# Four small edits to a planned attention and gated-FFN kernel: v transfers cut the other way, set-up work moved between engines, the pooled softmax scaled on ScalarE, the first block's weight remainders on VectorE

## The chip, the cores and the metric

One core of one Trainium2 chip runs the whole program. The time is device microseconds of one execution. The kernel before was timed three times: 1013.88, 1006.59 and 1011.54 us, median 1011.54 us. A profiled execution has a time of its own, and its trace is what the rows below come from.

## The reference, cut to what matters

```python
# q, k, v: [4 batches, 8 heads, 576 positions, 64], float32
q_d, k_d, v_d = means over groups of 4 positions            # 144 pooled positions
out_d  = softmax(q_d @ k_d.T / 8) @ v_d                      # pooled attention
out_up = repeat(out_d, 4 times along the positions)
scores = where(|i - j| < 4, q @ k.T / 8, -1e9)               # band of 7 positions
x = out_up + softmax(scores) @ v                             # -> [2304 tokens, 512]
x = (sigmoid(x @ w_gate) * (x @ w_val)) @ w_out              # 512 -> 1536 -> 512
h = x @ w_in                                                 # 512 -> 2048
out = (h * sigmoid(1.702 * h)) @ w_out2                      # 2048 -> 512
```

The weights come as 64-bit floats. All sums must hold float32 accuracy.

## The kernel before

The tokens are cut into five blocks: block b (0 to 3) is the first 512 positions of batch b, and block 4 gathers the last 64 of all four batches. TensorE multiplies in a fast format that does not hold a whole float32, so every operand of a dense product is split into a high part and a remainder ("hi" and "lo"), and each product is three matmuls (L710 to L712): hi by hi, lo by hi, hi by lo.

The work before each of blocks 0 to 3 is the attention of that batch, cut into four jobs (one for each pair of heads, `Job`). A job loads q and k transposed (`load`), pools them on GpSimd (`pool4`, L462 and L464), forms the scores of the band on TensorE (L494), does their softmax on VectorE and ScalarE (L501 to L521), and does the pooled attention: scores on TensorE (L534), maxima on VectorE (L541), exponentials with their sums on ScalarE (L549), the inverse of the sums on VectorE (L556, L557), the scaling by it on GpSimd (L561, two instructions a job, each of 72 x 288 elements), a transpose on TensorE against an identity matrix `ident` (L575), and a copy on ScalarE (L580). Then TensorE multiplies the band (L603) and the pooled part (L611) by the values, and `combine` makes the two parts of x.

Two jobs share one half of the value columns (`Values`, eight halves in all). A half is loaded twice. `vg` holds groups of four rows on 72 partitions, two transfers of 288 KB, and VectorE sums them (L431, L433). `vt` holds windows of 32 rows, 24 windows as 4 quarters of the partitions by 6 columns: window number 6i+g lies in partitions 32i to 32i+31, column g. It is loaded in six transfers: one for each quarter of the partitions (32 partitions by 6, or 5, columns), and one each for the first and the last window, which stand partly outside the sequence and are cut short.

The first layer's weights are made out of 64-bit words while block 0 is computed. For each of 36 tiles of 128 x 512, `bits` scales the upper words (L657 on VectorE for the first few, L659 on ScalarE after that), and shifts and joins the halves on VectorE (L661, L663); `signed` puts the sign in (L668, VectorE). The float32 tile stays on the chip. `parts_of` then makes the two parts: ScalarE rounds to hi (L674), and GpSimd or VectorE subtracts it (L676). In block 0 all 36 remainders are GpSimd's; in blocks 1 to 3 the third part of each step is VectorE's, and in block 4 every second tile.

The order is fixed when the program is built. Each piece of work is put down with its engine, a length in ns, what it reads and writes, and a due time (`op`); `Plan.order` walks through a simple model of five engines, gives each engine the ready piece that is due first, and emits the instructions in that order. Each engine runs its own instructions strictly in the order in which they were emitted, and the SP queue issues all the transfers in its order. Where the planner sees TensorE idle early, it puts in filler matmuls (L882).

The set-up at the start is not planned: `memset`s for padding and constants, a band mask made on GpSimd (L336 to L347), and `ident`, are emitted ahead of all planned work, in the order of the source.

Of the kernel before, what the change touches and what calls it, by code (L numbers as in the profile page):

```python
# [10 lines left out]
F32 = mybir.dt.float32  # L11
# [8 lines left out]
P = 128  # L20
# [41 lines left out]
class Plan:  # L62
# [29 lines left out]
    def op(self, eng, ns, fn, reads=(), writes=(), due=0.0, after=0.0):  # L92
        o = Op()
        o.eng, o.ns, o.fn, o.due, o.n, o.ready = eng, ns, fn, due, len(self.ops), after
        o.fresh, o.bufs = [], set()
        deps = set()
        for group, writing in ((reads, False), (writes, True)):
            for x in group:
                b, part = x if isinstance(x, tuple) else (x, None)
                assert b.some or b.slot.last is b  # L100
                if b.some:
                    o.bufs.add(b)
                    if not b.log:
                        o.fresh.append(b)
                new = True
                for p, q, w in b.log:
                    if (w or writing) and (part is None or q is None or part == q):
                        deps.add(p)
                        new = new and not w
                if new:  # L110
                    for x in b.before:
                        deps.update(e[0] for e in x.log)
        for group, writing in ((reads, False), (writes, True)):
            for x in group:
                b, part = x if isinstance(x, tuple) else (x, None)
                b.log.append((o, part, writing))
        deps.discard(o)
        o.deps = deps
        self.ops.append(o)
        return o  # L120
# [97 lines left out]
def tile_multiscale_attention_gated_ffn(  # L218
# [9 lines left out]
    nc = tc.nc  # L228
    B, NHP, _, S = qT.shape
    D = 64  # L230
    DM = v.shape[2]
# [3 lines left out]
    G = S // 4  # L235
    GH = G // 2
# [14 lines left out]
    NQ, NU = 24, 30  # L251
    NT = S // NQ
    NG = NT // 4
    VC = 2 * P
    HALF = S // 2

    sb = ctx.enter_context(tc.tile_pool(name="sb", bufs=1))
# [5 lines left out]
    op, buf = plan.op, plan.buf  # L263
# [13 lines left out]
    KPAD = 3  # L277
# [25 lines left out]
    qslots, kslots, vslots, pslots = (plan.rings[nm][0] for nm in ("qt", "kt", "vt", "pt"))  # L303
# [23 lines left out]
    warm = sb.tile([P, P], BF16, name="warm", tag="warm")  # L327
    nc.vector.memset(warm, 0.0)
    for s in qslots:
        nc.gpsimd.memset(s.t[:, S:], 0.0)  # L330
    for s in kslots:
        nc.gpsimd.memset(s.t[:, :KPAD], 0.0)
        nc.gpsimd.memset(s.t[:, KPAD + S:], 0.0)
    mask = sb.tile([P, NG, NU], F32, name="mask", tag="mask")
    band = sb.tile([P, NU], F32, name="band", tag="band")
    nc.gpsimd.memset(band, 0.0)  # L336
    for i in range(4):
# [7 lines left out]
                            fill=NEG, base=-3, channel_multiplier=0)  # L345
    nc.gpsimd.affine_select(out=mask[96:, NG - 1], in_=mask[96:, NG - 1], pattern=[[-1, NU]],
                            compare_op=ALU.is_ge, fill=NEG, base=S + 2 - NQ * (NT - 1), channel_multiplier=0)  # L347
    for s in vslots:
        nc.gpsimd.memset(s.t[:32, 0], 0.0)
        nc.gpsimd.memset(s.t[96:, NG - 1], 0.0)  # L350
    ident = sb.tile([P, P], F32, name="ident", tag="ident")
    make_identity(nc, ident)
    for s in pslots:
        nc.vector.memset(s.t, 0.0)


    def act_ns(n, psum=False):
# [8 lines left out]
    def dma(out_, in_, nbytes, reads, writes, due, after=0.0):  # L366
        op("sp", nbytes, lambda: nc.sync.dma_start(out=out_, in_=in_), reads, writes, due, after)
# [32 lines left out]
    class Values:  # L400
# [6 lines left out]
        def load(self):  # L407
            b, c = self.b, slice(self.c0, self.c0 + VC)
            self.vg, self.vt, self.vd = buf("vg"), buf("vt"), buf("vd")

            hp = self.job.hp
            d, after = (self.job.t0 - 3000.0, self.job.t0 - 12000.0) if b else (4500.0 * hp, 4500.0 * hp)
            for kh in range(2):
                dma(self.vg.t[:, kh], v[b, kh * 4 * GH:(kh + 1) * 4 * GH, c].rearrange("(g r) d -> g r d", r=4),
                    GH * 4 * VC * 4, [], [(self.vg, kh)], d, after)
            d, after = (self.job.due(0.2), self.job.t0 - 9000.0) if b else (4500.0 * hp + 3000.0, 6000.0 * hp)
            for i in range(4):
                g0, g1 = i == 0, NG - (i == 3)
                row = NQ * (NG * i + g0) - 3
                src = v[b, row:row + 32, c]  # L420
                src = bass.AP(tensor=src.tensor, offset=src.offset,
                              ap=[[DM, 32], [NQ * DM, g1 - g0], [1, VC]])
                dma(self.vt.t[32 * i:32 * i + 32, g0:g1], src, 32 * (g1 - g0) * VC * 4, [], [(self.vt, i)], d, after)
            dma(self.vt.t[3:NU, 0], v[b, :NU - 3, c], (NU - 3) * VC * 4, [], [(self.vt, 4)], d, after)
            row = NQ * (NT - 1) - 3
            dma(self.vt.t[96:96 + S - row, NG - 1], v[b, row:S, c], (S - row) * VC * 4, [], [(self.vt, 5)], d, after)

        def pool(self):
            vg, vd = self.vg, self.vd
# [6 lines left out]
    class Job:  # L436
# [88 lines left out]
        def down(self):  # L525


            ss = [Buf(None, self.banks) for _ in range(2)]
            qd, kd, nmd, smd, pd = self.qd, self.kd, self.nmd, self.smd, self.pd

            def pe():
                for r in range(2):
                    for h in range(2):
                        nc.tensor.matmul(ss[h].t[:GH, r * G:(r + 1) * G],  # L534
                                         qd.t[h * D:(h + 1) * D, r * GH:(r + 1) * GH],
                                         kd.t[h * D:(h + 1) * D, :], start=True, stop=True)

            at = self.due(0.5)
            op("pe", 560.0, pe, [qd, kd], [*ss, nmd, (smd, 0), (smd, 1), (pd, 0), (pd, 1)], at)
            for h in range(2):  # L540
                op("dve", dve_ns(2 * G), lambda h=h: nc.vector.reduce_max(  # L541
                    nmd.t[:, 2 * h:2 * h + 2], ss[h].t[:GH, :2 * G].rearrange("p (r k) -> p r k", k=G), axis=AX.X),
                   [ss[h]], [(nmd, h)], at)
            op("dve", 90.0, lambda: nc.vector.tensor_scalar_mul(nmd.t, nmd.t, -SCALE_D), [], [nmd], at)

            def ex(h):
                for r in range(2):
                    x = 2 * h + r
                    nc.scalar.activation(pd.t[:, h, r], ss[h].t[:GH, r * G:(r + 1) * G], AF.Exp,  # L549
                                         bias=nmd.t[:, x:x + 1], scale=SCALE_D, accum_out=smd.t[:, x:x + 1])  # L550

            for h in range(2):
                op("act", 1100.0, lambda h=h: ex(h), [nmd, ss[h]], [(pd, h), (smd, h)], at)

            def inv():
                nc.vector.tensor_scalar_add(smd.t, smd.t, 1.0e-9)  # L556
                nc.vector.reciprocal(smd.t, smd.t)  # L557

            op("dve", 305.0, inv, [], [smd], at)
            for h in range(2):  # L560
                op("pool", 680.0, lambda h=h: nc.gpsimd.tensor_mul(  # L561
                    pd.t[:, h], pd.t[:, h], smd.t[:, 2 * h:2 * h + 2, None].to_broadcast([GH, 2, G])),
                   [smd], [(pd, h)], at)

        def down_t(self):
            self.pdt = buf("pdt")
            ss = [Buf(None, self.banks) for _ in range(2)]
            pd, pdt = self.pd, self.pdt

            def pe():  # L570
                for h in range(2):
                    for kh in range(2):
                        for r in range(2):
                            o = kh * G + r * GH
                            nc.tensor.transpose(ss[h].t[:GH, o:o + GH], pd.t[:, h, r, kh * GH:(kh + 1) * GH],  # L575
                                                ident[:GH, :GH])

            op("pe", 500.0, pe, [(pd, 0), (pd, 1)], [*ss, (pdt, 0), (pdt, 1)], self.due(0.65))
            for h in range(2):
                op("act", 370.0, lambda h=h: nc.scalar.copy(  # L580
                    pdt.t[:, h], ss[h].t[:GH, :2 * G].rearrange("p (k q) -> p k q", q=G)),
                   [ss[h]], [(pdt, h)], self.due(0.65))
# [98 lines left out]
    def weights(vi, f, part, t):  # L681

        if vi["layer"] == 2:
            return wt[2, f, part]
        if vi["j"] == 0:
            w32[f, part] = buf("w")
            signed(*bits(1, f, part, t - 8000.0), w32[f, part], t - 8000.0)
        hi, lo = buf("whi"), buf("wlo")
        nsplit[0] += 1
        eng = "pool"  # L690
        if vi["j"] == E:
            eng = ("pool", "dve")[nsplit[0] % 2]
        elif vi["j"] > 0 and part == 2:
            eng = "dve"
        parts_of(w32[f, part], hi, lo, t - 4000.0, eng)
        return hi, lo
# [225 lines left out]
```

## Time and profile before

| | |
|---|---|
| three runs, median | 1011.54 us (1006.59 to 1013.88) |
| profiled execution, its own time | 1016.06 us |
| its span | 1014.2 us |
| TensorE busy | 970.4 us, 96% |
| VectorE busy | 524.7 us, 52% |
| ScalarE busy | 395.6 us, 39% |
| GpSimd busy | 309.1 us, 30% |
| mean granted TensorE clock | 0.967 of full speed |

Busy times are shares of the whole span, and the stages differ much: the attention and the making of the weights stand in the first fifth, the two layers' matmuls fill the rest. A row of a stage says more than the table. PE is TensorE's matmuls, PEld its weight loads, DVE VectorE, ACT ScalarE, POOL GpSimd, SP the queue that issues the transfers. In the chain of waits, "issue" is time in which an engine waited for nothing that the profile shows.

### The profile page before, as it was taken

To read this page: it belongs to the slowest core of one execution; us is meant where nothing else is said; L and a number is where in the kernel's file an instruction comes from. 1 tells how busy PE (TensorE), PEld (TensorE's weight loads), DVE (VectorE), ACT (ScalarE), POOL (GpSimd) and SP (SyncE) were. 2 spreads that over 40 slices of the span, in tenths; PEclk is the share of its full clock that TensorE was granted. 3 is DMA by queue.
4 is the path that set the end of the run, shared out by engine and by line. 5 is a ranking of instruction groups with operands and counts; after the bars stand their busy time and mean duration, and the time that the engine had idled before them with its cause. 6 is when DMAs were issued, how large, how long until landed. Compare 5 with 4: busy or idle time off the path is not lost.

```text
span 1014.2 us, 18484 instructions
## 1 busy us (share of the span) xinstructions
PE 970.4 (96%) x7614; PEld 790.8 (78%) x7614; DVE 524.7 (52%) x886; ACT 395.6 (39%) x822; POOL 309.1 (30%) x290
## 2 busy tenths in 40 slices
PE   6597998999999999999999989999999999999997
PEld 5575776787777877888888987788888788888886
DVE  5679999545453554467565679723222222322232
ACT  2334444444444443455555655423213221312222
POOL 5266454644434543345444442102001100100000
PEclk7679897999999999999999999999999999999999
DMA  8654844350012410124203225102000100100010
GB/s 186 169 165 130 220 151 145 80 141 29 4 50 56 119 32 8 44 76 166 84 1 110 96 76 184 55 1 83 1 1 23 51 1 1 52 1 1 0 43 21
DMA packets 37270, 72.42 MB, mean 71 GB/s; under 512 B 5777, under 2 KB 17985, under 8 KB 37185
## 3 DMA queue, kind: packets, MB, share of 16 engines
q1 hardware_dynamic: 37184, 71.24, 24.7%
q8 instruction: 60, 0.98, 0.4%
q14 instruction: 26, 0.20, 0.1%
HBM read 61.26 MB, written 9.96 MB: 70 GB/s over the span
## 4 chain that ended last, share of the span: by engine, by line
PE 79%; DVE 11%; issue 4%; DMA 2%; ACT 1%; POOL 1%; SPq 0%; POOLq 0%; DVEq 0%; ACTq 0%
PE ph L710 15%; PE ph L711 14%; PE ph L712 14%; PE acc L710 10%; PE acc L711 10%; PE acc L712 10%; DVE we L663 3%; PE pa L603 2%; DMA vg<-v 2%; DVE we L668 1%; DVE we L661 1%; DVE w L668 1%; PE pa L534 1%; PE pa L494 1%; DMA w<-w 1%
## 5 line engine op out<-in xcount | busy, mean ns | idle before, releaser
L676 POOL TENSOR_TENSOR wlo<-w,whi 128x512 fp32r<-128x512 f32 x126 | 178.8, 1422 | 242.0 <-ACT whi L674 224.9
L746 DVE SCALAR_TENSOR_TENSOR th<-th,ph 128x512 f32<-128x512 f32 (+1 forms) x140 | 88.5, 632 | 303.9 <-ACT th L741 206.5
L710 PE MATMUL ph<-xhi,whi 128*128 128x512 f32 (+1 forms) x480 | 185.0, 386 | 3.4 <-ACT th L741 3.2
L711 PE MATMUL ph<-xhi,wlo 128*128 128x512 f32 (+1 forms) x480 | 181.0, 377 | 1.0 <-POOL wlo L676 1.0
L712 PE MATMUL ph<-xlo,whi 128*128 128x512 f32 (+1 forms) x480 | 180.4, 376 | 0.0
L741 ACT ACTIVATE th<-ph 128x512 f32<-128x512 f32 (+1 forms) x140 | 77.6, 554 | 256.3 <-PE ph L712 256.3
L674 ACT CAST whi<-w 128x512 fp32r<-128x512 f32 x180 | 111.1, 617 | 124.1 <-PE acc L712 54.0
L710 PE MATMUL ph<-xhi,w 128*128 128x512 f32 (+1 forms) x320 | 120.4, 376 | 1.1 <-DVE th L746 0.8
L750 DVE TENSOR_TENSOR glo<-th,ghi 128x512 fp32r<-128x512 f32 (+1 forms) x140 | 95.6, 683 | 48.7 <-ACT ghi L749 47.9
L711 PE MATMUL ph<-xhi,w 128*128 128x512 f32 (+1 forms) x320 | 119.3, 373 | 0.0
L712 PE MATMUL ph<-xlo,w 128*128 128x512 f32 (+1 forms) x320 | 119.2, 373 | 0.0
L711 PE MATMUL acc<-w,glo 128*128 128x512 f32 x288 | 114.7, 398 | 1.1 <-DVE glo L750 1.1
L710 PE MATMUL acc<-w,ghi 128*128 128x512 f32 x288 | 114.2, 397 | 1.5 <-ACT ghi L749 1.5
L712 PE MATMUL acc<-w,ghi 128*128 128x512 f32 x288 | 114.5, 397 | 0.0
L710 PEld LDWEIGHTS ph<-xhi,whi 128*128 128x128 f32 x480 | 92.7, 193 | 22.9 <-issue 3.9
L712 PEld LDWEIGHTS ph<-xlo,whi 128*128 128x128 f32 x480 | 92.8, 193 | 16.4 <-DVE xlo L637 0.2
L711 PEld LDWEIGHTS ph<-xhi,wlo 128*128 128x128 f32 x480 | 92.7, 193 | 15.7 <-POOL wlo L676 1.4
L749 ACT CAST ghi<-th 128x512 fp32r<-128x512 f32 (+1 forms) x140 | 80.6, 576 | 58.7 <-DVE th L746 56.2
L821 POOL TENSOR_TENSOR xlo<-st,xhi 128x512 fp32r<-128x512 f32 (+1 forms) x24 | 29.1, 1230 | 224.8 <-ACT xhi L819 224.8
L710 PE MATMUL acc<-ghi,whi 128*128 128x512 f32 (+1 forms) x240 | 90.8, 378 | 0.6 <-DVE ev L786 0.6
L711 PE MATMUL acc<-ghi,wlo 128*128 128x512 f32 (+1 forms) x240 | 88.7, 370 | 0.0
L712 PE MATMUL acc<-glo,whi 128*128 128x512 f32 (+1 forms) x240 | 88.4, 368 | 0.0
(99 smaller groups left out, 1305.4 us busy)
## 6 DMA issues: line engine op xcount, KB each, us to landing
w<-w SPq DMA_DIRECT2D x68, 512.0 KB
qt<-qT SPq DMA_DIRECT2D x16, 288.0 KB
kt<-kT SPq DMA_DIRECT2D x16, 288.0 KB
vg<-v SPq DMA_DIRECT2D x16, 288.0 KB
x2d<-ev SPq DMA_DIRECT2D x16, 256.0 KB
st<-x2d SPq DMA_DIRECT2D x16, 256.0 KB
out<-ev SPq DMA_DIRECT2D x16, 256.0 KB
vt<-v SPq DMA_DIRECT2D x16, 192.0 KB
```

The source lines that it names most:

```text
L603: nc.tensor.matmul(s.t[h * D:(h + 1) * D, q:q + NQ], vt.t[ks, g, v0 + h * D:v0 + (h + 1) * D], tt.t[ks, h, g, :NQ], start=True, stop=True, ...
L663: op("dve", 602.0, lambda: nc.vector.scalar_tensor_tensor(e.t, wv[:, :, 0], 29, e.t, op0=ALU.logical_shift_right, op1=ALU.bitwise_or), [w] ...
L674: op("act", 520.0, lambda: nc.scalar.copy(hi.t, m.t.bitcast(F32)), [m], [hi], due)
L676: op(eng, ns, lambda: on.tensor_sub(lo.t, m.t.bitcast(F32), hi.t.bitcast(F32)), [m, hi], [lo], due)
L710: nc.tensor.matmul(o, lhi, rhi, start=first, stop=False)
L711: nc.tensor.matmul(o, llo, rhi, start=False, stop=False)
L712: nc.tensor.matmul(o, lhi, rlo, start=False, stop=last)
L741: op("act", act_ns(n, True), lambda h=h: nc.scalar.activation(th.t[:, :n], h.t[:, :n], AF.Tanh, scale=0.5 if layer == 1 else 1.702 / 4.0), ...
L746: op("dve", dve_ns(n), lambda: nc.vector.scalar_tensor_tensor(th.t[:, :n], th.t[:, :n], 1.0, hb[-1].t[:, :n], op0=ALU.add, op1=ALU.mult), ...
L749: op("act", act_ns(n), lambda: nc.scalar.copy(gh.t[:, :n], th.t[:, :n]), [th], [gh], t)
L750: op("dve", dve_ns(n), lambda: nc.vector.tensor_sub(gl.t[:, :n], th.t[:, :n], gh.t[:, :n].bitcast(F32)), [th, gh], [gl], t)
L821: op("pool", pool_ns(n), lambda k=k, st=st: nc.gpsimd.tensor_sub(lo.t[:, k, :n], st.t[:, :n], hi.t[:, k, :n].bitcast(F32)), [st, (hi, k)], ...
```

## The change

Five places are touched.

1. The small `memset`s of the padding of q, k and v go from GpSimd to VectorE, and those of `pt` stand with them ahead of the mask.
2. `ident` becomes a planned piece of GpSimd's work with an early due time; until now it stood in the set-up. The transposes now read it as a planned buffer.
3. The four transfers of `vt` by quarters of the partitions become six by columns: each fills one column g on all 128 partitions (96 for the first and the last column). The two short ones stay. A half goes from six transfers of `vt` to eight, with the same bytes.
4. The scaling of the pooled softmax goes from two GpSimd instructions a job to four ScalarE instructions, each of 72 x 144 elements with one scale for each partition.
5. In block 0 all 36 remainders of the weights go from GpSimd to VectorE.

```diff
     for s in qslots:
-        nc.gpsimd.memset(s.t[:, S:], 0.0)
+        nc.vector.memset(s.t[:, S:], 0.0)
     for s in kslots:
-        nc.gpsimd.memset(s.t[:, :KPAD], 0.0)
-        nc.gpsimd.memset(s.t[:, KPAD + S:], 0.0)
+        nc.vector.memset(s.t[:, :KPAD], 0.0)
+        nc.vector.memset(s.t[:, KPAD + S:], 0.0)
+    for s in vslots:
+        nc.vector.memset(s.t[:32, 0], 0.0)
+        nc.vector.memset(s.t[96:, NG - 1], 0.0)
+    for s in pslots:
+        nc.vector.memset(s.t, 0.0)
...
-    for s in vslots:
-        nc.gpsimd.memset(s.t[:32, 0], 0.0)
-        nc.gpsimd.memset(s.t[96:, NG - 1], 0.0)
-    ident = sb.tile([P, P], F32, name="ident", tag="ident")
-    make_identity(nc, ident)
-    for s in pslots:
-        nc.vector.memset(s.t, 0.0)
+    ident = Buf(Slot(sb.tile([P, P], F32, name="ident", tag="ident")))
+    op("pool", 650.0, lambda: make_identity(nc, ident.t), [], [ident], -10.0e3)
...
-            for i in range(4):
-                g0, g1 = i == 0, NG - (i == 3)
-                row = NQ * (NG * i + g0) - 3
-                src = v[b, row:row + 32, c]
+            for g in range(NG):
+                i0, i1 = g == 0, 4 - (g == NG - 1)
+                src = v[b, NQ * (NG * i0 + g) - 3:NQ * (NG * i0 + g) + 29, c]
                 src = bass.AP(tensor=src.tensor, offset=src.offset,
-                              ap=[[DM, 32], [NQ * DM, g1 - g0], [1, VC]])
-                dma(self.vt.t[32 * i:32 * i + 32, g0:g1], src, 32 * (g1 - g0) * VC * 4, [], [(self.vt, i)], d, after)
+                              ap=[[NG * NQ * DM, i1 - i0], [DM, 32], [1, VC]])
+                dma(self.vt.t[32 * i0:32 * i1, g], src, 32 * (i1 - i0) * VC * 4, [], [(self.vt, g)], d, after)
...
+            def norm(h):
+                for r in range(2):
+                    x = 2 * h + r
+                    nc.scalar.mul(pd.t[:, h, r], pd.t[:, h, r], smd.t[:, x:x + 1])
+
             for h in range(2):
-                op("pool", 680.0, lambda h=h: nc.gpsimd.tensor_mul(
-                    pd.t[:, h], pd.t[:, h], smd.t[:, 2 * h:2 * h + 2, None].to_broadcast([GH, 2, G])),
-                   [smd], [(pd, h)], at)
+                op("act", 640.0, lambda h=h: norm(h), [smd], [(pd, h)], at)
...
         eng = "pool"
         if vi["j"] == E:
             eng = ("pool", "dve")[nsplit[0] % 2]
-        elif vi["j"] > 0 and part == 2:
+        elif vi["j"] == 0 or part == 2:
             eng = "dve"
```

## Rows read from the trace of the kernel before

**Rows 1.** Windows: us, each engine's busy time, granted clock, DMA share, GB/s.

```profile
0.00:57.00 57.00, 37.12 (x989) 32.16 (x989) 32.67 (x84) 16.20 (x55) 28.93 (x58) 0.69 0.76 186
70.00:180.00 110.00, 96.83 (x959) 75.03 (x959) 107.30 (x167) 53.73 (x116) 57.74 (x45) 0.91 0.55 160
200.00:300.00 100.00, 100.00 (x1153) 79.78 (x1153) 49.60 (x101) 42.53 (x98) 40.76 (x39) 1.00 0.19 48
```

**Rows 2.** Chain that ended last: start us, us, what; first 57 us.

```profile
10.83 5.11 issue
...
25.60 5.19 issue
...
33.28 3.71 issue
...
50.11 4.69 POOL pd L561
```

**Rows 3.** Windows between those waits, columns as in the first group.

```profile
0.00:10.80 10.80, 7.42 (x222) 6.76 (x223) 2.35 (x7) 1.28 (x1) 8.72 (x36) 0.87 0.86 190
10.80:25.60 14.80, 9.69 (x254) 8.27 (x251) 10.64 (x27) 5.03 (x21) 6.46 (x11) 0.63 0.90 184
25.60:33.30 7.70, 2.49 (x129) 2.31 (x128) 4.13 (x8) 0.63 (x2) 1.87 (x2) 0.69 1.06 289
```

**Rows 4.** Page: TensorE's line, and the instruction queue (packets, MB, share).

```profile
PE 970.4 (96%) x7614; PEld 790.8 (78%) x7614; DVE 524.7 (52%) x886; ACT 395.6 (39%) x822; POOL 309.1 (30%) x290
...
q8 instruction: 60, 0.98, 0.4%
```

**Rows 5.** Transfers by issue: queue, count, KB each.

```profile
vg<-v SPq DMA_DIRECT2D x16, 288.0 KB
...
vt<-v SPq DMA_DIRECT2D x16, 192.0 KB
```

**Rows 6.** Windows: two vg transfers alone; then vg and vt together.

```profile
41.00:43.00 2.00, 2.00 (x26) 1.62 (x22) 1.10 (x3) 0.00 (x0) 0.00 (x0) 0.69 0.74 218
...
108.50:113.50 5.00, 5.00 (x116) 3.76 (x115) 4.93 (x7) 1.59 (x3) 4.00 (x5) 1.00 1.05 149
```

**Rows 7.** Timeline: SP issues four weight tiles; VectorE first reads one.

```profile
22.75 4.96 SPq L367 DMA_DIRECT2D w<-w  x4
...
43.85 0.77 DVE L657 TENSOR_SCALAR we<-w 128x512 f32<-128x512 f32 x2
```

**Rows 8.** ScalarE by line, 57 to 190 us: busy us, mean ns, idle.

```profile
L549 ACT ACTIVATE pd<-pa,nmd 72x144 f32<-72x144 f32 x16 | 5.8, 371 | 4.3 <-DVE nmd L544 4.3
```

**Rows 9.** Timeline of GpSimd's set-up: first vt memset, first pooling.

```profile
4.21 0.30 POOL L349 MEMSET vt<- 32x256 f32 x1
...
6.17 0.67 POOL L462 TENSOR_TENSOR half<-qt 128x288 f32<-128x288 f32 x1
```

**Rows 10.** GpSimd and VectorE by line, 57 to 190 us.

```profile
L676 POOL TENSOR_TENSOR wlo<-w,whi 128x512 fp32r<-128x512 f32 x33 | 51.0, 1554 | 50.5 <-ACT whi L674 36.6 <-DVE th L746 7.7 <-DVE xlo L637 5.0
...
L668 DVE SCALAR_TENSOR_TENSOR w<-w,we 128x512 int32<-128x512 int32 x33 | 28.4, 860 | 0.2
L663 DVE SCALAR_TENSOR_TENSOR we<-w,we 128x512 int32<-128x512 int32 x33 | 27.7, 838 | 0.3
L661 DVE TENSOR_SCALAR we<-we 128x512 int32<-128x512 int32 x33 | 24.6, 746 | 0.7 <-ACT we L659 0.6
```

**Rows 11.** VectorE by line, 190 to 440 us.

```profile
L676 DVE TENSOR_TENSOR wlo<-w,whi 128x512 fp32r<-128x512 f32 x23 | 18.6, 807 | 0.0
...
L663 DVE SCALAR_TENSOR_TENSOR we<-w,we 128x512 int32<-128x512 int32 x1 | 0.7, 693 | 0.0
L661 DVE TENSOR_SCALAR we<-we 128x512 int32<-128x512 int32 x1 | 0.4, 427 | 0.5 <-ACT we L659 0.5
```

**Rows 12.** Waits, whole span (total, times, longest); ScalarE's cast, 57 to 190.

```profile
DVE wlo L676 <- ACT whi L674: 15.5, 13, 4.0
...
L674 ACT CAST whi<-w 128x512 fp32r<-128x512 f32 x33 | 20.3, 615 | 23.6 <-DVE w L668 14.0 <-PE ph L712 5.5 <-PE acc L712 4.1
```

More of the change, by code (lines that the diff above doesn't have):

```diff
@@ L416, in load @@
             d, after = (self.job.due(0.2), self.job.t0 - 9000.0) if b else (4500.0 * hp + 3000.0, 6000.0 * hp)
-            for i in range(4):
-                g0, g1 = i == 0, NG - (i == 3)
-                row = NQ * (NG * i + g0) - 3
-                src = v[b, row:row + 32, c]
+            for g in range(NG):
+                i0, i1 = g == 0, 4 - (g == NG - 1)
+                src = v[b, NQ * (NG * i0 + g) - 3:NQ * (NG * i0 + g) + 29, c]
                 src = bass.AP(tensor=src.tensor, offset=src.offset,
-                              ap=[[DM, 32], [NQ * DM, g1 - g0], [1, VC]])
-                dma(self.vt.t[32 * i:32 * i + 32, g0:g1], src, 32 * (g1 - g0) * VC * 4, [], [(self.vt, i)], d, after)
-            dma(self.vt.t[3:NU, 0], v[b, :NU - 3, c], (NU - 3) * VC * 4, [], [(self.vt, 4)], d, after)
+                              ap=[[NG * NQ * DM, i1 - i0], [DM, 32], [1, VC]])
+                dma(self.vt.t[32 * i0:32 * i1, g], src, 32 * (i1 - i0) * VC * 4, [], [(self.vt, g)], d, after)
+            dma(self.vt.t[3:NU, 0], v[b, :NU - 3, c], (NU - 3) * VC * 4, [], [(self.vt, NG)], d, after)
             row = NQ * (NT - 1) - 3
-            dma(self.vt.t[96:96 + S - row, NG - 1], v[b, row:S, c], (S - row) * VC * 4, [], [(self.vt, 5)], d, after)
+            dma(self.vt.t[96:96 + S - row, NG - 1], v[b, row:S, c], (S - row) * VC * 4, [], [(self.vt, NG + 1)],
+                d, after)
         def pool(self):
@@ L575, in pe @@
                             nc.tensor.transpose(ss[h].t[:GH, o:o + GH], pd.t[:, h, r, kh * GH:(kh + 1) * GH],
-                                                ident[:GH, :GH])
-            op("pe", 500.0, pe, [(pd, 0), (pd, 1)], [*ss, (pdt, 0), (pdt, 1)], self.due(0.65))
+                                                ident.t[:GH, :GH])
+            op("pe", 500.0, pe, [(pd, 0), (pd, 1), ident], [*ss, (pdt, 0), (pdt, 1)], self.due(0.65))
             for h in range(2):
```

## The prediction

> **What bounds the kernel now.** I read the windows by stage first. From 200 us on TensorE is busy 100.00 of 100 us at full clock, so whatever is won or lost before that is carried to the end unchanged [rows 1]. From 70 to 180 us VectorE is busy 107.30 of 110 us and TensorE 96.83: VectorE sets the pace there, and TensorE could save at most 13.2 us of idling. In the first 57 us no engine is full: TensorE works 37.12 us, VectorE 32.67. So there are two bounds, a start that waits, and a stage that VectorE fills.
>
> What the start waits for is in the chain of waits: three pieces called "issue", 5.11, 5.19 and 3.71 us, 14.0 in all, in which TensorE waits for no other engine, and then a scaling on GpSimd, 4.69 us [rows 2]. Up to the first wait TensorE ran 222 + 223 instructions, up to the second 505 more, up to the third 257 more [rows 3]: steps of about 256. The page has 60 transfers of instructions of 0.98 MB / 60 = 16 KB, one for (7614 + 7614) / 60 = 254 of TensorE's instructions [rows 4]. I read the waits as TensorE out of instructions, whose next block is a transfer that queues with the data: the DMA share was 0.86 to 1.06 ahead of them [rows 3]. The rows don't name the reason; this reading is mine.
>
> **The v transfers.** A half of v is two transfers of 288 KB and six of `vt` [rows 5], 704 KB and two short ones of 27 KB: 1.36 MB. While vg and vt ran together the core moved 149 GB/s at a share of 1.05; two vg transfers alone 218 GB/s at 0.74, so a busy engine moved nearly twice as much [rows 6]. I take it that four transfers which each write 32 partitions get in each other's way, and that writing all 128 undoes this. At 149 GB/s a half takes 9.1 us, at 218 / 0.74 = 295 GB/s 4.6 us. The first two waits each stand behind one half, so each loses 4.5 us at most; I take 4 each, **-8 us**, near the upper rate, since the new transfers write all partitions as vg writes most. The third wait stands behind the weights, which this change leaves alone: 0. Bounds: all three waits gone, -14; nothing gained, 0; a loss is the second rival. SP issues two more transfers a half; four weight issues took 4.96 us, so each of these is 1.2 us at most, 2.5 a half, 5 for the two early halves. Queued behind them are the first weights, issued at 22.75 and first read at 43.85 [rows 7]: that slack covers it.
>
> **The pooled scaling.** It moves to ScalarE as four instructions a job of 72 x 144. The nearest row, the exponential of the same shape, takes 371 ns [rows 8]: 1.5 us a job. In the chain it replaces 4.69 us [rows 2]: **-3 us**, once, for the last job ahead of block 0's matmuls. The other jobs lie beside VectorE's full stage or behind the waits: 0. ScalarE has room (53.73 of 110) [rows 1]. Should it be busy with a cast as the scaling comes, 0.6 us are lost; bounds -4.7 to 0.
>
> **The set-up.** GpSimd's memsets of v and the identity lie between 4.21 and 6.17 us, where its first pooling starts [rows 9]; that pooling can start some 2 us earlier. What follows runs into the first wait, which ends when the instructions arrive and not when TensorE gets there: 0, bounds -2 to 0. VectorE takes ten small memsets in a time when it has nothing else (1.2 us at 0.1 to 0.3 each). The planned identity costs GpSimd the same 0.5 us, before a transpose that needs it much later: 0.
>
> **The remainders.** This is the part that could cost most. VectorE gets 36 subtractions. One took 807 ns with GpSimd at work beside it; a lone instruction of the same size with two inputs took 693 [rows 11]. In the full stage it is 33 x 0.693 = 22.9 us more. But the same 33 instructions of GpSimd, 1554 ns each, vanish, and VectorE's own were longer beside them: L668 860, L663 838, L661 746 ns [rows 10], against 693, 693 and 427 lone [rows 11]. That is 167 + 145 + 319 = 631 ns a tile, 20.8 us for 33. Net **+2 us**. Bounds: no relief and the dear price, 36 x 0.807 = +29; all of TensorE's idling in the stage recovered, -13. I take the middle value since both halves of it come from the same instructions.
>
> **Sum:** -8 - 3 + 0 + 2 = -9 to -10; I take -10, as other VectorE forms, not in these rows, are lengthened too. The profiled execution took 1016.06 us, 4.5 more than the median; so 1006 on its scale, and 1011.5 - 10 = **1001.5 us** on that of the runs. Below about 1% (10.1 us) a measurement here can't be told from no change.
>
> **Rivals.**
>
> *The waits stay.* If the instruction blocks come late for a reason other than v's transfers, only the scaling and the remainders count: -3 + 2 = -1, 1010.5 us. For it: the third wait came at a time without v in its queue. Against it: the first two fell in the fullest DMA windows [rows 3]. By the Trainium skill (Runtime: NRT & Kernel Launch, Instruction fetch mechanics) instructions are streamed in blocks of 16 KiB and crossing a block is mostly hidden; by that rule the term of -8 would be 0. The block size agrees with rows 4; the 14 us of rows 2 speak against "hidden" here. Chance 0.20.
>
> *The new transfers use few engines.* Two vg transfers alone kept 0.74 x 16 = 11.8 engines busy, not 16 [rows 6], so a transfer needn't use all. The new source pattern has 4 (or 3) as its first count. If a transfer ran on so many engines at 218 / 11.8 = 18.4 GB/s each, four of 131 KB would take 1.8 us each and two of 98 KB on three engines 1.8 each: 10.7 us after vg's 2.7, 13.4 instead of 9.1. If the instruction blocks rode on those engines, two waits would grow by 4.3 us instead of shrinking by 4: -10 + 16.6 = +6.6, 1018 us. If they rode on others, they would be freed sooner and the forecast holds. The Trainium skill (DMA: Bandwidth & Descriptors, how many engines) says that a transfer runs on the largest number up to 16 that divides the slowest count of both sides; that is 12 for vg's 72 partitions, and the 11.8 agree. By it the new transfers use 4 or 3 engines. No row says on which engine the instructions come. Chance of the bad branch 0.16.
>
> *The remainders wait for their cast*, the case on the slow side. A remainder needs ScalarE's rounding, 615 ns, and VectorE runs in order: where it waits, everything behind it does. VectorE's remainders waited 15.5 us in 13 cases, up to 4.0 us [rows 12], 0.29 us for each of 54 (three blocks of 12 and half of the 36 of block 4), in stages where VectorE had time. If each of 36 waits for one whole cast, it is 22.1 us: -10 + 22 = +12, 1023.5 us. It eats the gain from 0.28 us a remainder on, and shows as slower from 0.56 on. Against it: the due times put the making of a tile 4 us ahead of its split (L687, L695). Chance 0.14.
>
> **Chances.** The forecast has 0.50. Its own range is -4 to -20 (991.5 to 1007.5). What is left out of the sum (the third wait, the set-up once the first wait is short, other lengthened VectorE forms) is all gain, so I put 0.33 of it beyond -10.1 and 0.17 within. The waits that stay: 0.03 and 0.17. Few engines: 0.10 within, 0.06 slower. The cast: 0.02 and 0.12. So faster 0.36, within 1% 0.46, slower 0.18. The range from 990 to 1020 takes in the first three cases and leaves out the worse half of the last and a larger gain.
>
> **What would show it.** In the profile after, the three pieces of "issue" should come to 6 us rather than 14, with the share of the DMA engines or the time of a half of v lower. The scaling should be four ScalarE instructions of about 0.37 us and no longer in the chain. VectorE should stay above 95% busy from about 60 to 170 us, with L661 near 0.43 and L663 and L668 near 0.69 us, and 36 new remainders near 0.69. I am wrong if VectorE shows gaps that end with the cast, if the first weights are late for VectorE, or if the issue pieces are as long as before. If TensorE's busy share in that stage rises well over 90%, the stage was worth more than I gave it.

## The result, and the profile after

The kernel after took 1000.59 us (median of 7 runs, 998.96 to 1002.12) against 1011.54: a ratio of 0.9898, 95% interval 0.9871 to 0.9924, 10.3 us less by the ratio. The forecast was 1001.5. The sum was right and two of its four terms had the wrong sign: the v transfers cost time here instead of saving it, and the remainders, booked as a small loss, are the largest gain. The kernel after with the v transfers of before takes 989.47 us; it is the best version here that computes the reference.

The profiled execution took 1000.16 us with a span of 998.1. Its page gives the engines' busy times, to be read beside [rows 4]; GpSimd's fell from 309.1 to 219.1 us, VectorE's hardly moved. The two profiled executions are 15.9 us apart (1016.06 and 1000.16), some 5 more than the medians, so their rows overstate the gain by that much.

```profile
PE 961.1 (96%) x7611; PEld 782.6 (78%) x7611; DVE 526.0 (53%) x932; ACT 414.1 (41%) x886; POOL 219.1 (22%) x212
```

The windows of the kernel after (columns as in [rows 1]):

```profile
0.00:57.00 57.00, 40.76 (x1089) 35.20 (x1089) 39.03 (x107) 22.48 (x75) 14.66 (x38) 0.82 0.63 190
70.00:180.00 110.00, 100.74 (x1099) 77.12 (x1098) 102.42 (x204) 63.61 (x148) 15.10 (x14) 0.98 0.56 174
200.00:300.00 100.00, 100.00 (x1030) 79.73 (x1029) 47.24 (x93) 47.85 (x120) 34.47 (x32) 1.00 0.20 59
```

From 200 us on TensorE is as full as before, so the whole gain is made earlier. From 70 to 180 us it idles 110 - 100.74 = 9.3 us instead of 13.2, and VectorE is at 93%, no longer at 98%. The granted clock rose too, from 0.69 to 0.82 in the first 57 us and from 0.91 to 0.98 from 70 to 180. With practically the same matmuls TensorE's busy time fell by 9.3 us over the whole span and its idle time by 6.8, so the larger part of the difference between the two profiles is matmuls that ran at a higher clock, the smaller part waits that are gone. What the start waits for is in the chain of the first 57 us (start, length, what):

```profile
3.68 6.01 DMA vg<-v
...
14.59 6.92 DMA kt<-kT
...
29.17 0.68 issue
...
33.90 7.87 DMA x1d<-xf
```

Where [rows 2] had 14.0 us of "issue" the chain has one piece of 0.68, and in its place stand transfers. The chain shows only what ended last; all of TensorE's waits in that time (total, times, longest) hold 2.8 + 1.6 + 0.7 = 5.1 us of "issue", and 6.1 us for one transfer of k:

```profile
PE acc L494 <- DMA kt<-kT: 6.1, 1, 6.1
...
PE acc L494 <- issue: 2.8, 1, 2.8
PE pa L606 <- issue: 1.6, 1, 1.6
...
PE acc L606 <- issue: 0.7, 1, 0.7
```

Why the transfers are late is in the timeline of SP, which issues them in order (start, time to issue, what, how many):

```profile
4.53 9.50 SPq L367 DMA_DIRECT2D vt<-v  x8
14.14 0.36 SPq L367 DMA_DIRECT2D qt<-qT  x1
14.59 0.38 SPq L367 DMA_DIRECT2D kt<-kT  x1
...
20.02 8.86 SPq L367 DMA_DIRECT2D vt<-v  x8
28.93 3.28 SPq L367 DMA_DIRECT2D w<-w  x4
```

Eight transfers of `vt` hold SP for 9.50 us, and what stands behind them waits: q and k of the next jobs until 14.14, the first weights until 28.93 ([rows 7]: 22.75). The same happens late in block 0, where a weight tile stands behind five of them:

```profile
159.52 6.91 SPq L367 DMA_DIRECT2D vt<-v  x5
166.53 1.30 SPq L367 DMA_DIRECT2D w<-w  x1
```

It lands some 9.5 us later, ScalarE's scaling of its words (L662) waits for it, and VectorE stands still behind that:

```profile
176.76 0.43 DVE L664 TENSOR_SCALAR we<-we 128x512 int32<-128x512 int32 x1 [3.89 <-ACT we L662]
```

The forms of VectorE from 57 to 190 us, which answer to [rows 10] (busy us, mean ns, idle before):

```profile
L671 DVE SCALAR_TENSOR_TENSOR w<-w,we 128x512 int32<-128x512 int32 x32 | 24.2, 756 | 0.1
L679 DVE TENSOR_TENSOR wlo<-w,whi 128x512 fp32r<-128x512 f32 x33 | 23.8, 720 | 0.1
L666 DVE SCALAR_TENSOR_TENSOR we<-w,we 128x512 int32<-128x512 int32 x32 | 22.0, 686 | 0.0
L664 DVE TENSOR_SCALAR we<-we 128x512 int32<-128x512 int32 x32 | 13.8, 432 | 6.8 <-ACT we L662 6.8
```

The three old forms fell from 860, 838 and 746 ns to 756, 686 and 432, and the new remainders take 720. The scaling on ScalarE, beside [rows 8]:

```profile
L563 ACT ACTIVATE pd<-pd,smd 72x144 f32<-72x144 f32 x16 | 5.4, 414 | 0.3 <-DVE smd L557 0.3
```

### The profile page after: what moved, and what is told of

Read it like the earlier page. It is cut to its first block, busy times and chain, and to the rows that moved or that the text cites. A ratio compares the mean times of both kernels' runs of the same rounds, so it can differ in the third digit from the quotient of the medians.

```text
span 998.1 us, 18490 instructions
## 1 busy us (share of the span) xinstructions
PE 961.1 (96%) x7611; PEld 782.6 (78%) x7611; DVE 526.0 (53%) x932; ACT 414.1 (41%) x886; POOL 219.1 (22%) x212
## 3 DMA queue, kind: packets, MB, share of 16 engines
q1 hardware_dynamic: 36848, 71.23, 22.9%
## 4 chain that ended last, share of the span: by engine, by line
PE 78%; DVE 13%; DMA 5%; issue 2%; ACT 1%; SPq 0%; DVEq 0%; ACTq 0%
PE ph L713 15%; PE ph L714 14%; PE ph L715 14%; PE acc L713 10%; PE acc L714 10%; PE acc L715 10%; DMA w<-w 3%; DVE we L666 3%; PE pa L606 2%; DVE we L671 2%; DVE w L671 1%; DVE we L664 1%; DVE wlo L679 1%; PE pa L494 1%; DMA x1d<-xf 1%
## 5 line engine op out<-in xcount | busy, mean ns | idle before, releaser
L713 PE MATMUL ph<-xhi,whi 128*128 128x512 f32 (+1 forms) x480 | 183.0, 381 | 0.4 <-ACT th L744 0.4
L714 PE MATMUL ph<-xhi,wlo 128*128 128x512 f32 (+1 forms) x480 | 178.9, 373 | 2.0 <-DVE wlo L679 2.0
L715 PE MATMUL ph<-xlo,whi 128*128 128x512 f32 (+1 forms) x480 | 177.9, 371 | 0.0
L679 POOL TENSOR_TENSOR wlo<-w,whi 128x512 fp32r<-128x512 f32 x90 | 121.1, 1345 | 239.2 <-ACT whi L677 234.7
L713 PE MATMUL ph<-xhi,w 128*128 128x512 f32 (+1 forms) x320 | 120.0, 375 | 1.1 <-DVE th L749 0.9
L713 PE MATMUL acc<-w,ghi 128*128 128x512 f32 x288 | 113.9, 396 | 1.5 <-ACT ghi L752 1.5
L713 PEld LDWEIGHTS ph<-xhi,whi 128*128 128x128 f32 x480 | 91.1, 190 | 19.0 <-issue 3.9
L713 PE MATMUL acc<-ghi,whi 128*128 128x512 f32 (+1 forms) x240 | 91.0, 379 | 1.0 <-DVE ev L789 0.6
L679 DVE TENSOR_TENSOR wlo<-w,whi 128x512 fp32r<-128x512 f32 x90 | 69.4, 772 | 19.2 <-ACT whi L677 19.1
```

The source lines that it names most:

```text
L679: op(eng, ns, lambda: on.tensor_sub(lo.t, m.t.bitcast(F32), hi.t.bitcast(F32)), [m, hi], [lo], due)
L713: nc.tensor.matmul(o, lhi, rhi, start=first, stop=False)
L714: nc.tensor.matmul(o, llo, rhi, start=False, stop=False)
L715: nc.tensor.matmul(o, lhi, rlo, start=False, stop=last)
```

## The experiments

Each was timed in five rounds beside the kernel before, whose median was 1010.27, 1012.24 and 1011.48 us in the three groups (the kernel after beside 1011.54); the ratio to it is what is compared. "Alone" is an edit put into the kernel before, "undone" one taken out of the kernel after.

| kernel | median us | ratio to before, 95% interval |
|---|---|---|
| after | 1000.59 | 0.9898 (0.9871 to 0.9924) |
| after, v transfers undone | 989.47 | 0.9812 (0.9777 to 0.9847) |
| after, v transfers undone but in the first batch | 995.73 | 0.9850 (0.9816 to 0.9884) |
| after, remainders undone | 1006.40 | 0.9962 (0.9944 to 0.9980) |
| after, scaling undone | 1002.52 | 0.9919 (0.9888 to 0.9950) |
| after, vt from consecutive rows | 983.47 | 0.9728 (0.9699 to 0.9758) |
| v transfers alone | 1010.79 | 0.9993 (0.9978 to 1.0007) |
| remainders alone | 1001.87 | 0.9890 (0.9865 to 0.9915) |
| set-up alone | 1011.53 | 0.9994 (0.9978 to 1.0010) |
| scaling alone | 1004.25 | 0.9934 (0.9914 to 0.9955) |
| remainders and scaling | 997.17 | 0.9854 (0.9823 to 0.9886) |
| columns on ScalarE's queue, first batch | 999.65 | 0.9883 (0.9860 to 0.9906) |
| quarters on ScalarE's queue, first batch | 997.41 | 0.9865 (0.9845 to 0.9884) |

**1. The v transfers undone.**

```diff
-            for g in range(NG):
...
+            for i in range(4):
...
```

> The kernel after with one part undone: vt is loaded by quarters of the partitions again, everything else stays changed. Theory A (the new v transfers shorten the waits for instructions at the start, 14.0 us before and 4.8 us after in the chain's pieces over 2 us and their like): the waits come back, the first dense matmul moves from 49.0 back to about 55 us, and the total lies at 1005 to 1009 us. Rival B (the new transfers cost as much as they save, since SP is held 9.5 us at each half and weights land late at 90 to 109 and 166 to 176 us): the start gets worse but the late weights go, and the total lies at 994 to 1001 us.

989.47 us, 11 less than the kernel after (9 by the ratios), and less than either theory expected. The new transfers cost time. The second theory expected a worse start without them; it got better, with the first matmul of L713 at 46.6 us against 49.0. SP in this kernel:

```profile
4.51 3.67 SPq L367 DMA_DIRECT2D vt<-v  x6
10.14 0.35 SPq L367 DMA_DIRECT2D qt<-qT  x1
...
17.19 2.72 SPq L367 DMA_DIRECT2D vt<-v  x6
22.16 4.32 SPq L367 DMA_DIRECT2D w<-w  x4
```

A half of `vt` holds SP for 3.67 and 2.72 us instead of 9.50 and 8.86, and the first weights leave 6.8 us sooner. Late weights don't all go: from 52 to 206 us ScalarE still waits 8.4 us for weights (10.6 in the kernel after), but VectorE behind it only 2.4 instead of 6.8. TensorE's waits for instructions in the first 57 us are short here with quarters too, 3.1 + 1.1 + 0.6 = 4.8 us, so the columns had little to shorten in this company.

**2. The new transfers in the first batch alone.**

```diff
+            if b == 0:
+                for g in range(NG):
...
+            else:
+                for i in range(4):
...
```

> The kernel after with the new v transfers for batch 0 alone (two halves of eight); the other six are loaded by quarters of the partitions. If the gain of the new transfers lies at the start and their cost in the late weights of block 0: the first dense matmul stays near 49 us, the waits of 9.6, 7.8 and 9.5 us for weights shrink to under 3 each, and the total is 990 to 997 us. If the late weights cost nothing in the end, since TensorE had run ahead: 999 to 1002 us. If the quarters delay the weights as much: the same as the kernel after or slower.

995.73 us, about the middle: by the medians 6 us of the cost arise in the first batch and 5 in the later ones, but its interval overlaps with both neighbours', so the split is rough. The first dense matmul starts at 52.2 us, not near 49 as expected. In the start TensorE waited 10.1 us for one transfer of k.

**3. The same columns, read from consecutive rows.** The destination, the bytes and the number of transfers are those of the kernel after; the source is one run of rows, so that its first count is 128 (or 96) and not 4 (or 3). It leaves out the gather of the right windows, so its values are not the reference's; it is there for its time.

```diff
-                              ap=[[NG * NQ * DM, i1 - i0], [DM, 32], [1, VC]])
+                              ap=[[DM, 32 * (i1 - i0)], [1, VC]])
```

> The kernel after with the same vt transfers in number, bytes, size of a run and destination (one column on 128 or 96 partitions each), but from consecutive rows of v, so that the source's first count is 128 or 96 and not 4 or 3. It loads other rows than the reference needs, so its values differ. Theory D (the new transfers lose because their source begins with a count of 4, which leaves them 4 or 3 DMA engines): the late weights and SP's long issues go, a vt issue takes 0.4 us and not 1.2, the total is 984 to 991 us, at or below the 989.5 of the kernel with quarters. Rival E (they lose by being eight instead of six, or by writing all partitions): 998 to 1002 us, like the kernel after.

983.47 us, 17 less than the kernel after. The first count of the source decides, as far as this can show it. The windows from 8.0 to 13.5 us show how (second last column: share of the 16 DMA engines; last: GB/s). The kernel after:

```profile
8.00:13.50 5.50, 2.75 (x79) 2.10 (x68) 4.18 (x12) 0.98 (x4) 1.15 (x3) 0.82 0.34 102
```

From consecutive rows:

```profile
8.00:13.50 5.50, 2.71 (x87) 2.28 (x78) 4.23 (x12) 1.00 (x4) 1.64 (x4) 0.93 0.98 266
```

By quarters, the kernel of experiment 1:

```profile
8.00:13.50 5.50, 4.42 (x128) 3.81 (x129) 1.83 (x4) 0.00 (x0) 1.15 (x3) 0.75 1.06 176
```

With a first count of 4 the mean is 0.34 x 16 = 5.4 engines and 102 GB/s, the end of vg (until 9.69) and other transfers counted in; with 128, all of them and 266. The Trainium skill (DMA: Bandwidth & Descriptors, how many engines) has the number of engines as the largest up to 16 that divides the slowest count of both sides, so 4 and 16 here; the shares of 0.34 and 0.98 agree, as far as a window with other transfers in it can. The quarters keep 16 engines busy too but move 176 GB/s, which fits the prediction's premise that four transfers of 32 partitions get in each other's way. The consecutive rows gain 6 us over the quarters (989.47 to 983.47; 8 by the ratios). That is near the 8 forecast for columns, but it does not come the forecast way: TensorE's waits for instructions are longer here than with quarters (8.9 against 4.8 us). A run of rows also reads DRAM in another order; what that is worth apart from the count was not tested.

**4. The v transfers alone.**

```diff
-            for i in range(4):
...
+            for g in range(NG):
...
```

> The kernel before with one part done: the new v transfers alone. My prediction: -8 us, 1002 us, with the first two waits for instructions short. Since undoing this part in the kernel after won 11 us, theory D expects a loss here as well: 1011 to 1018 us against 1010.3, with SP held at each half; the first waits may still shrink.

1010.79 us: nothing gained, nothing lost. TensorE's waits in the first 57 us (total, times, longest) say part of why:

```profile
PE acc L494 <- DMA kt<-kT: 4.2, 1, 4.2
...
PE acc L494 <- issue: 1.4, 1, 1.4
...
PE pa L494 <- DMA kt<-kT: 0.9, 1, 0.9
PE pa L494 <- issue: 0.5, 1, 0.5
...
PE acc L603 <- issue: 0.2, 1, 0.2
```

The three waits for instructions shrank from 14.0 us to about 2, and 5.1 us of waiting for k came in their place: SP issues the next q at 12.68 instead of 10.12. That leaves a gain at the start, and the stage takes back more than half of it: the first matmul of L710 starts at 52.7 instead of 57.5 us, block 0's first layer ends at 204.0 instead of 206.1, and ScalarE waits 6.6 us for weights in between, 2.6 before. So the columns cost nothing alone and 9 to 11 us in company; what makes that difference is shown only in part (experiment 1).

**5. The remainders alone, and undone.**

```diff
-        elif vi["j"] > 0 and part == 2:
+        elif vi["j"] == 0 or part == 2:
```

> The kernel before with one part done: block 0's remainders on VectorE alone. My prediction: +2 us (1012 us), VectorE's busy time in the stage the same. Theory F (the move frees VectorE of about 23 us of lengthened instructions, and TensorE gets its remainders sooner than from GpSimd, so the stage ends earlier): 998 to 1004 us, with the first dense matmul unmoved at 57 us and the gain between the 50th and the 300th.

> The kernel after with one part undone: the remainders of block 0 go back to GpSimd. My prediction put the move to VectorE at +2 us, so by it this kernel is 2 us faster than the one after: 996 to 1000 us, with VectorE's L664, L666 and L671 lengthened again by some 20 us in the stage. Rival C (the move is the larger part of the gain, since the first 300 dense matmuls gained 16 us after the start's 8.6): 1005 to 1012 us.

Alone 1001.87 us, a gain of 11 by the ratio (9 to 14); undone, the kernel after loses 6 of its 10. VectorE from 57 to 190 us with the remainders alone:

```profile
L676 DVE TENSOR_TENSOR wlo<-w,whi 128x512 fp32r<-128x512 f32 x35 | 25.6, 731 | 0.1
L668 DVE SCALAR_TENSOR_TENSOR w<-w,we 128x512 int32<-128x512 int32 x34 | 25.3, 745 | 0.1
L663 DVE SCALAR_TENSOR_TENSOR we<-w,we 128x512 int32<-128x512 int32 x33 | 23.9, 724 | 0.0
L661 DVE TENSOR_SCALAR we<-we 128x512 int32<-128x512 int32 x33 | 14.3, 434 | 0.6 <-ACT we L659 0.6
```

The price is near the forecast, 25.6 us for 35 (22.9 for 33), and the three forms gave back (860 - 745) + (838 - 724) + (746 - 434) = 541 ns a tile, 17.9 us. Yet VectorE finishes the last tile of block 0 sooner, with the subtractions in its queue. The last L668 of the kernel before:

```profile
185.03 0.68 DVE L668 SCALAR_TENSOR_TENSOR w<-w,we 128x512 int32<-128x512 int32 x1
```

and with the remainders alone:

```profile
180.62 1.75 DVE L668 SCALAR_TENSOR_TENSOR w<-w,we 128x512 int32<-128x512 int32 x1
...
185.56 0.69 DVE L676 TENSOR_TENSOR wlo<-w,whi 128x512 fp32r<-128x512 f32 x1
```

So some 4 us are VectorE's own. Counted through the trace, the 432nd matmul of L710 to L712 after the first, where block 0's first layer ends, starts at 195.7 instead of 206.1 us: 15.0 us behind the start of that instruction, and 21.1 before. The first of these matmuls starts only 1.0 us sooner (56.5 against 57.5), so the gain is made in the stage. The other 6 us are not a faster way of the remainders to TensorE, which hardly waited for them before either. Its waits from 57 to 206 us before, and then with the remainders alone:

```profile
PE pa L575 <- POOL pd L561: 9.0, 5, 4.2
...
PE ph L711 <- POOL wlo L676: 1.0, 1, 1.0
```

```profile
PE pa L575 <- DVE sc L501: 4.7, 4, 2.7
PE ph L711 <- DVE wlo L676: 1.2, 3, 0.6
```

The wait for the pooled scaling is gone, though the scaling is still GpSimd's; the same matmuls now wait 4.7 us for VectorE. A wait of TensorE for the scaling stands in all five profiled kernels whose remainders are GpSimd's (7.1 to 10.2 us, the scaling on GpSimd or on ScalarE) and in none of the nine whose remainders are VectorE's; why the scaling is late beside remainders on GpSimd is not shown. The windows from the first of the matmuls counted to the 432nd after it, before and with the remainders alone (columns as in [rows 1]), show the sum:

```profile
57.50:206.10 148.60, 135.20 (x1338) 105.32 (x1335) 129.84 (x211) 68.62 (x151) 80.06 (x62) 0.91 0.51 144
```

```profile
56.50:195.70 139.20, 132.93 (x1432) 102.29 (x1429) 128.97 (x256) 69.03 (x153) 32.19 (x27) 0.95 0.56 154
```

TensorE idles 6.3 us in it instead of 13.4, and its mean granted clock is 0.95 instead of 0.91; how the 6 us divide between the two is open.

**6. The scaling alone, and undone.**

```diff
-                op("pool", 680.0, lambda h=h: nc.gpsimd.tensor_mul(
+                op("act", 640.0, lambda h=h: norm(h), [smd], [(pd, h)], at)
```

> The kernel before with one edit: the pooled softmax is scaled on ScalarE. Remainders alone gave -10, set-up alone 0, v transfers alone 0, yet all but the v transfers together gave -22. Theory 1: the missing 10 us are the scaling's own, because GpSimd's turn at it holds the transposes of every job: about 1001, ratio 0.990. Theory 2: the scaling alone gives what the chain of the kernel before shows for it, 3 to 5 us at most: 1007 to 1009; the rest comes only once the remainders are gone from GpSimd. Theory 3: alone it gives nothing, since the stage behind it is filled by VectorE: 1011 to 1013.

> The kernel after with one part undone: the pooled softmax is scaled on GpSimd again. My prediction: 3 us slower than the kernel after, 1002 to 1005 us, with one scaling of 2 to 5 us back in the chain ahead of block 0. Rival: nothing (998 to 1002 us), since GpSimd is idle there once the remainders are gone and the scaling takes its lone 0.65 us an instruction.

Alone 1004.25 us, 6.7 less (4.6 to 8.7); undone 1002.52, against 1000.59, inside the noise. The first lies between the ranges of its first two theories, and the second can't tell its two expectations apart. The 9.0 us that TensorE waited for the scaling in the full stage (experiment 5) had been passed over by the prediction. With the scaling on ScalarE that wait is only a little shorter, now for ScalarE's part:

```profile
PE pa L578 <- ACT pd L563: 7.1, 3, 3.6
```

The rest of its gain lies ahead of the stage: the first matmul of L713 starts at 49.2 us, 8.3 sooner. The 4.69 us of [rows 2] are gone, and "issue" is 1.70 + 2.56 + 4.90 = 9.2 us instead of 14.0. That second part can't be put down to the scaling (see the last section).

**7. The set-up alone, and the other two without it.**

```diff
-        nc.gpsimd.memset(s.t[:, S:], 0.0)
+        nc.vector.memset(s.t[:, S:], 0.0)
...
+    op("pool", 650.0, lambda: make_identity(nc, ident.t), [], [ident], -10.0e3)
```

> The kernel before with one part done: the set-up edits alone. My prediction: 0 us (1008 to 1012), since the first wait for instructions ends when they arrive. Rival G (the start is a chain whose head is GpSimd's first pooling, and the waits for instructions come and go with the moment at which a block is asked for): the three issue pieces of 5.1, 5.2 and 3.7 us change, and the total falls by 4 to 10 us, to 1000 to 1006.

> The kernel before with two edits: the remainders on VectorE and the scaling on ScalarE; set-up and v transfers as before. Theory 1: these two are the whole gain of the kernel after without its v transfers: 989 to 991. Theory 2: the set-up edits, worth nothing alone, count once the other two are in (GpSimd or VectorE start earlier): 995 to 1000. If it stands at 1000 to 1002 the scaling adds nothing to the remainders.

Alone 1011.53 us, nothing. Remainders and scaling together are 997.17; with the set-up as well, which is experiment 1, it is 989.47. That is 8 us by the medians and 4 by the ratios, whose intervals overlap, so a gain of the set-up in company is likely but its size is open.

**8. `vt` of the first batch on ScalarE's queue, by columns and by quarters.** These were to tell SP's time apart from the time of the data.

```diff
+    def adma(out_, in_, nbytes, reads, writes, due, after=0.0):
+        op("act", 60.0, lambda: nc.scalar.dma_start(out=out_, in_=in_), reads, writes, due, after)
...
+            if b == 0:
...
```

> The kernel after with the new v transfers for the first batch only, as the run that took 995.7, but for that batch ScalarE's queue issues vt and not SP. Theory 1: the new transfers cost by holding SP, behind which q, k and the first weights stand: with SP free it comes to 989 to 992. Theory 2: the cost is the data itself, four engines that carry vt and keep q, k and the weights waiting on them whoever issues: 995 to 997 again. Theory 3: ScalarE is held in SP's place, and its exponentials and casts are late: 998 or more.

> The control of the run before: the kernel after with vt by quarters in all batches, and in the first batch vt is issued by ScalarE's queue. The quarters hold SP only 3.67 and 2.72 us a half, so moving them gives SP some 6 us: 987 to 990 if SP's time is what counts, 989.5 as with SP if it is not, 992 or more if ScalarE's time for six issues a half counts.

999.65 and 997.41 us: the control fails too, so they settle nothing. ScalarE's queue does not stand behind SP's first transfers and starts `vt` at once. In the run by columns it is held itself, its own first work starts at 10.40 us, and vg is late on SP. First ScalarE's queue, then SP's:

```profile
0.73 9.63 ACTq L370 DMA_DIRECT2D vt<-v  x8
```

```profile
11.04 2.31 SPq L367 DMA_DIRECT2D vg<-v  x2
```

Whether the time lies in SP being held or in the four engines that everything else must share stays open; in all five kernels whose first batch has columns on four engines, issued by SP, the two came together.

## Why the prediction was right, and where it was not

The forecast of 10 us less held by luck, through two errors that cancel. Alone, the four parts measure -0.7, -6.7, -0.6 and -11 us, -19 together, and experiment 1, which has the last three, measures -19. That agreement is rough, since remainders and scaling together measure -15 and not -18. The columns then take back 9 to 11.

**The v transfers (-8).** The reading of the chain held: the waits for instructions did shrink, by more than the 4 us each that were forecast (14.0 to about 2 alone). The reason given for it did not: the instruction blocks came sooner not beside faster transfers but beside transfers that leave two thirds of the engines idle. With all 16 engines on the same number of transfers they were late again (last section). The step that failed is the one after: "SP issues two more transfers a half ... each of these is 1.2 us at most, 2.5 a half, 5 for the two early halves. Queued behind them are the first weights ... that slack covers it." It priced two transfers more, where all eight became dear: SP is held 6.3 us longer in the first half (9.50 against 3.19 for six in the kernel before) and 6.1 in the second (8.86 against 2.73). Eight on all engines (experiment 3) hold it 5.48 and 6.43, so the two more were priced about right, and the other 4.0 and 2.4 us come with the few engines. And it named the weights alone, for which the slack nearly sufficed: VectorE first reads one at 37.13 us, after a wait of 1.3. But q and k of the next jobs stand between the two halves: TensorE's wait for k is 6.1 us in the kernel after. This is the second rival's mechanism, with its 18 GB/s an engine (102 / 5.4 = 19), but not its place: it put the loss on the instruction blocks, which were the part that gained, as its other branch had it (that they ride on other engines and are freed sooner). It priced 4.3 us more a half for the data; SP was held 6 longer.

**The remainders (+2).** The price was right (0.731 us each, 0.693 forecast). The step that failed is the "middle value" that set 20.8 us of relief against 22.9 and stopped there. Left out were TensorE's own delays in that stage, which come and go with GpSimd's remainders: 9.0 us of waiting for the pooled scaling and a granted clock of 0.91, where the remainders alone leave none of that wait and a clock of 0.95. VectorE's own part of the gain, some 4 us, is more than the sum of the rows shown gives; other lengthened forms, which the sum named and did not count, got shorter too (L431 from 2312 to 1212 ns, L544 from 573 to 165). The lower bound, -13, was the right end. The rival by which they wait for their cast did not come: the row of L679 above has 0.1 us of idle time ahead of 33 remainders.

**The scaling (-3).** Right in sign; alone it measures twice that, undone within noise of it. That "the other jobs lie beside VectorE's full stage or behind the waits: 0" passed over 9.0 us of waiting there, of which this move took little and the remainders' move all. Its instructions take 414 ns, not 371.

**The waits stay**, the first rival, did not come either, though where `vt` reads with 16 engines (experiment 3) TensorE waited 3.8 + 2.8 + 2.3 = 8.9 us for instructions again, and that is the fastest kernel of all: those waits alone were not what the time hung on.

**The set-up (0).** Right alone. GpSimd's first pooling did move, from 6.17 to 3.99 us in the kernel after.

**What the profile should show.** The "issue" pieces went to 5.1 us (0.68 in the chain), below the 6 named. L664 and L666 came out at 0.432 and 0.686 as forecast, L671 at 0.756. From 60 to 170 us both engines are as full as the prediction asked:

```profile
60.00:170.00 110.00, 105.45 (x1128) 81.19 (x1125) 106.28 (x216) 64.88 (x149) 15.47 (x16) 1.00 0.58 178
```

VectorE is at 97%, and TensorE at 96%, well over the 90% that were to show that the stage was worth more than booked, and it was. VectorE's longest gap comes right behind, at 173 to 177 us, and ends with ScalarE's work on a late weight tile: not the first weights that the prediction named as a sign of being wrong, but the same queue.

## What to carry to other kernels

Before a transfer is cut another way, read the first count on both sides: 128 partitions on one side bring nothing if the other side's first count is 4. Price the queue's issue time for every transfer of the new kind, and list everything that stands behind them in that queue, up to the next thing that an engine waits for. And judge the parts of a change one by one: this one passes as 1% faster, and without the v transfers it is 1.9% faster.

## What the runs showed of the hardware

The length of the first wait for instructions is not a property of the kernel alone. With the scaling alone it begins at 10.81 us, after 75 matmuls of L494, and is short:

```profile
12.51 0.43 PE L494 MATMUL acc<-kt,qt 64*32 64x30 f32 x21 [1.70 <-issue]
```

With scaling and remainders, whose first ten us are the same work, it begins at 10.17 and is as long as before:

```profile
15.35 0.42 PE L494 MATMUL acc<-kt,qt 64*32 64x30 f32 x21 [5.18 <-issue]
```

and with the set-up as well TensorE gets there at 8.82:

```profile
9.90 0.32 PE L494 MATMUL acc<-kt,qt 64*32 64x30 f32 x21 [1.08 <-issue]
```

By the Trainium skill (Runtime: NRT & Kernel Launch, Instruction fetch mechanics) crossing a block is mostly hidden; these waits of 1.08 to 5.18 us speak against that here, as [rows 2] did.

One profiled execution therefore can't say what an edit does to these waits, and single executions of these kernels with `vt` by quarters spread widely (991.33 to 1000.95 us with remainders and scaling, 988.45 to 996.5 in experiment 1), while those of the kernel after lie within 3.2 us. In the four profiled kernels with columns whose waits were read beside the kernel after (alone, remainders undone, scaling undone, first batch only) none of these waits was above 2.6 us, and the wait for k was 4.2 to 10.1.

The trace also has the transfers that bring TensorE's instructions, 16 KB each. In the kernel before, one lies inside each of the three waits of [rows 2]: they start at 12.90, 27.80 and 34.51 us and take 1.29, 1.70 and 1.07, and TensorE goes on 1.3 to 1.8 us after each has ended. So the prediction's reading of these waits as waits for instructions, which the rows did not show, holds. What differs between executions is the start and not the length: in the wait of 1.70 us above the transfer starts at 9.90 and takes 1.33, in that of 5.18 it starts at 12.56 and takes 1.32.

Counted from TensorE's entry into the block before, the transfers that belong to the second and third wait start 1.0 to 1.4 and at most 0.3 us later in the five kernels whose columns run on few engines, 3.1 to 7.0 and 3.0 to 4.7 later in the six with quarters, and 3.9 and 3.8 later in experiment 3, where as many transfers run on all engines (in each case with `vt` on SP's queue). For the first wait the groups overlap (0.9 to 2.9, 1.7 to 7.2, and 2.4). That fits transfers that stand behind busy engines; on which engines they run the trace does not say. The one after these starts later with the columns (4.8 to 6.5 us, 2.0 to 5.0 with quarters), and TensorE waited up to 1.8 us for it.
